# One attention head group of layer 1 as columns in every batch row, with one-piece copies, half-wise query spreading, earlier weight tails and new engine orders

## The chip, the core and the metric

The kernel runs on one core of a Trainium2 chip. The core has a matrix engine (TensorE, PE in the profile; its weight loads are PEld), a vector engine (VectorE, DVE), a scalar engine (ScalarE, ACT), GpSimd (POOL), and a sync engine (SyncE, SP) that here only starts DMA transfers. The engines run their own instruction streams in order and meet at semaphores. Matrix results go to PSUM, eight banks of 128 x 512 f32; all else lies in SBUF with 128 partitions.

The metric is the time of one execution on the device, in microseconds (us). A program is run several times; the median is compared.

## What is computed

Two layers, each attention over a cache and then a feed-forward block, with the same weights and the same cache in both layers. Eight batch rows, one token each, D = 448, 16 query heads on 8 cache heads ("kvh"), head size 256, and a window of the last 1024 of 4096 cached keys.

```python
def _A_ref(x, k_cache, v_cache, wq, wo):
    B, Sq, D = x.shape
    Hq, Dh = 16, 256
    Hkv, Sk = k_cache.shape[1], k_cache.shape[2]
    W = min(4096, max(256, Sk // 4))
    rep = Hq // Hkv
    q = (x @ wq).reshape(B, Sq, Hq, Dh).transpose(0, 2, 1, 3)
    k = jnp.repeat(k_cache[:, :, Sk - W:, :], rep, axis=1)
    v = jnp.repeat(v_cache[:, :, Sk - W:, :], rep, axis=1)
    scores = jnp.einsum("bhqd,bhkd->bhqk", q, k) * (Dh ** -0.5)
    o = jnp.einsum("bhqk,bhkd->bhqd", _softmax(scores), v)
    return o.transpose(0, 2, 1, 3).reshape(B, Sq, Hq * Dh) @ wo
...
x = A_x
x = x + _A_ref(_layernorm(x), A_k_cache, A_v_cache, A_wq, A_wo)
x = x + silu(_layernorm(x) @ B_w1) @ B_w2
x = x + _A_ref(_layernorm(x), A_k_cache, A_v_cache, A_wq, A_wo)
x = x + silu(_layernorm(x) @ B_w1) @ B_w2
```

## The kernel before

**Loads.** A batch row needs 8 K blocks and 8 V blocks, one of 512 KB for each kvh. They go through a ring of 30 SBUF slots, all started by SP in a fixed order (`pump`, `load_kv`, line 446): K 0 to 7 of row 0, V 0 to 7, K of row 1 and so on. Load n may start once the block 30 loads earlier has been read for the last time. Layer 2 uses the same blocks, so K block k of row b comes free when row b's layer-2 scores have read it, and the loads that wait for the first four K blocks of row b are V 6 and V 7 of row b+1 and K 0 and K 1 of row b+2. The weights are loaded once: `load_wq` (three pieces and a tail of 64 + 64 partitions), then `load_w2` and `load_wo` behind K of row 0, `load_w1` with its tail behind V of row 0. The tails are two DMAs each (`load_tail`, line 389). The input `x` is started by ACT.

**A batch row.** In what follows a name with @b is the work of row b.

- Layer 1: VectorE transposes the K blocks in place (line 599, names KW0 to KW7). `scores(b, 0, k2)` (line 614, S0.0 and S0.1, four groups of eight matmuls each for kvh 0 to 3 and 4 to 7), `softmax` (max0, exp0, perm0, turn0, l0, rl0), then the values. `pv_rows1` does kvh 0 to 3 (line 669, PV0), `pv_tiles1` kvh 4 to 7 one by one (line 680, PV4 to PV7). Each of the two ends in `o_turn`: ACT copies the PSUM bank (line 650, oev0, oevt), four matmuls turn it (line 651, oT0, oTt), VectorE scales it by the softmax sums (line 654, oTev0, oTevt). `wo_rows` (line 742, four groups of eight matmuls) multiplies with `wo` into bank XB; ACT copies the result row (line 776, rowb1), `fold` (line 481) turns it into columns and adds it to the residual in bank YB, and `xcols` (line 785, xb1) makes the layer's output x.
- `chain(b)`: statistics (line 793), `up` (line 806, w1), the second product (line 886, w2), copy (rowb2), fold, xb2, statistics; then `query_rows` makes the layer-2 queries: `wq` matmuls (line 858), a transpose on VectorE (line 511, qT), a product with a mask (line 865, qm), four matmuls that spread them (line 869, qd), two ACT copies (line 874, qbd2.0 and qbd2.1).
- Layer 2: `scores(b, 1, k2)` (also line 614, S1.0 and S1.1), softmax, `pv_rows2` (line 720, PV1.0 and PV1.1), `o_turn` (oev1, oT1, oTev1). What follows layer-2 attention is done for rows 0 to 6 together in `final_rows` and for row 7 in `final_last`.

**Row 7 is special before the change** (`LAST`). Its kvh 7 of layer 1 doesn't go through `pv_tiles1`. `pv_cols1` (line 691, PVc) multiplies the V block as weights, so that the result stands in columns at once, VectorE scales it (line 696, oTc7), and `wo_cols` (lines 758 and 760, woc, 24 matmuls) adds it straight to the residual in YB, with no copy, no turn and no fold. And its row copies are split: ACT copies a first part, VectorE the rest (`row_out`, lines 769 to 772; `o_turn`, lines 646 and 648). The planner lets a reader of a PSUM bank wait for earlier readers of that bank on other engines, so the VectorE part starts after the ACT part:

```python
for k in reads:
    ...
    if k[0] == "bank":
        for r in self.readers.get(k, ()):
            if r.eng != eng:
                dep(r, False)
```

**Order.** `Plan` keeps the tasks in program order, and for each engine the string in `ORDER` says which of the remaining tasks comes next: a digit n takes the n-th remaining one. SP has no string; it follows program order. `IDLE` says how many idle matmuls (line 848, 128 x 512, result unused) stand ahead of each row's `chain` and query spreading. Decoded, PE's order from layer-2 scores of row 5 to the statistics of row 6 is:

```
S1.0@5 x4  S1.1@5 x4  perm0@6 l0@6  PV0@6 x2  PV4@6  l1@5 perm1@5  oT0@6  PV5@6
PV1.0@5 x2  PV6@6  PV1.1@5  PV7@6  wo@6 x2  oTt@6  PV1.1@5  wo@6 x2  oT1@5
fold1@6  stat1@6
```

## Time and profile before

| what | us |
|---|---|
| median of 3 runs (lowest, highest) | 234.12 (233.54, 236.55) |
| the profiled execution | 234.68 |
| its span, first to last instruction | 232.9 |
| PE busy | 166.7 |
| DVE busy | 149.9 |
| ACT busy | 66.6 |
| POOL busy | 22.8 |

The profiled execution took 234.68 us, of which 232.9 lie between its first and its last instruction. PE busy counts matmuls, which are pipelined: 72% busy isn't 72% of what the engine could do. The page cuts the span in 40 slices of 5.8 us and gives for each the busy tenths of each engine, the matrix engine's granted clock, and the DMA share and rate. The timeline view lists instructions with start, duration, engine, line, output and input, and in brackets how long the engine had been idle and what released it. The windows view gives busy time by stretch, then the granted clock, the DMA share and GB/s.

### The profile page before, as it was taken

What the parts mean: (1) busy time and instruction counts of PE and PEld (TensorE: products, weight loads), DVE (VectorE), ACT (ScalarE), POOL (GpSimd) and SP (SyncE); (2) the same over time, 40 slices, a digit from 0 to 9 for tenths busy, and PEclk for the clock granted to TensorE, in tenths of its full rate; (3) what the DMA queues carried; (4) which work ended last, traced back from release to release, by engine and by line L of the source; (5) the groups of instructions that cost most, each with busy time, mean ns of one, the idle gap of its engine ahead of it and who ended that gap; (6) DMA issues with size and microseconds to landing.
All of it is one profiled execution on the core that took longest, in us unless ns stands there. A gap on an engine that the chain in (4) does not pass through costs nothing.

```text
span 232.9 us, 7828 instructions
## 1 busy us (share of the span) xinstructions
PE 166.7 (72%) x3479; PEld 97.3 (42%) x3479; DVE 149.9 (64%) x356; ACT 66.6 (29%) x188; POOL 22.8 (10%) x41
## 2 busy tenths in 40 slices
PE   0000338197988888878786978889788889898885
PEld 0000334135354545354335534453545455466644
DVE  6328986996963994297358736951984596424742
ACT  2000153631223326232222223223323223223331
POOL 1000202011000200110011002001100200000200
PEclk9999999769799999999999999999999999999999
DMA  6999999999999998999999999999999999500000
GB/s 246 377 377 404 378 380 403 410 374 396 405 393 404 407 408 336 343 418 406 348 385 416 406 349 414 407 390 389 409 406 379 412 407 408 221 3 3 3 3 4
DMA packets 22631, 78.17 MB, mean 336 GB/s; under 512 B 2231, under 2 KB 5318, under 8 KB 22214
## 3 DMA queue, kind: packets, MB, share of 16 engines
q1 hardware_dynamic: 22582, 77.68, 86.1%
q8 instruction: 27, 0.44, 0.8%
q14 instruction: 6, 0.05, 0.1%
q10 hardware_dynamic: 16, 0.01, 0.0%
HBM read 77.67 MB, written 0.01 MB: 334 GB/s over the span
## 4 chain that ended last, share of the span: by engine, by line
PE 35%; DVE 23%; DMA 18%; SPq 17%; ACT 3%; issue 2%; DVEq 0%; ACTq 0%
DVE slot L599 15%; DMA slot<-in_A_k_cache_dram 15%; SPq L446 10%; PE bank L614 9%; PE bank L806 5%; SPq L404 4%; PE bank L720 4%; DMA slot<-in_A_v_cache_dram 3%; PE bank L669 3%; SPq L389 3%; PE bank L680 2%; PE bank L742 2%; PE bank L869 2%; DVE bank L511 1%; DVE mm L626 1%
## 5 line engine op out<-in xcount | busy, mean ns | idle before, releaser
L599 DVE STREAM_TRANSPOSE slot<-slot 128x1024 uint32<-128x1024 uint32 x64 | 76.8, 1226 | 9.7 <-DMA slot<-in_A_k_cache_dram 9.5
L614 PE MATMUL bank<-slot,qbd 128*8 128x256 bf16 (+1 forms) x1024 | 38.4, 285 | 2.1 <-POOL qbd L590 1.1
L614 PEld LDWEIGHTS bank<-slot,qbd 128*8 128x8 bf16 (+1 forms) x1024 | 26.1, 88 | 13.3 <-DVE slot L599 4.2
L799 POOL TENSOR_TENSOR fcols<-fcols 128x1 f32<-128x1 f32 x17 | 9.4, 554 | 103.2 <-ACT fcols L797 103.2
L654 DVE TENSOR_TENSOR q1s<-bank,q1s 128x16 bf16<-128x16 f32 (+2 forms) x25 | 4.3, 171 | 22.8 <-PE bank L651 22.7
L806 PE MATMUL bank<-xz,w_sb 128*128 128x56 bf16 (+1 forms) x522 | 17.5, 191 | 0.0
L742 PE MATMUL bank<-wo_sb,q1s 128*1 128x449 bf16 x284 | 16.8, 354 | 0.6 <-DVE spread L374 0.5
L626 DVE TENSOR_REDUCE mm<-bank 128x1 f32<-128x256 f32 x17 | 7.2, 424 | 15.0 <-PE bank L614 14.8
L590 POOL TENSOR_TENSOR qbd<-q1s,fcols 128x256 bf16<-128x256 bf16 x16 | 9.6, 614 | 70.5 <-PE bank L680 62.4
L650 ACT ACTIVATE obuf<-bank 128x512 bf16<-128x512 f32 x15 | 9.0, 597 | 25.5 <-PE bank L680 18.1
L806 PEld LDWEIGHTS bank<-xz,w_sb 128*128 128x128 bf16 (+1 forms) x522 | 15.9, 99 | 0.7
L720 PE MATMUL bank<-slot,qbd 128*8 128x512 bf16 (+1 forms) x224 | 16.2, 381 | 0.0
L858 PE MATMUL bank<-wq_sb,xz 128*2 128x512 bf16 x196 | 13.7, 390 | 2.3 <-DVE xz L785 2.1
L633 ACT ACTIVATE qbd<-bank,mm 128x256 bf16<-128x256 f32 x17 | 8.1, 474 | 21.4 <-DVE mm L630 18.3
L669 PE MATMUL bank<-slot,qbd 128*4 128x512 bf16 x128 | 9.2, 410 | 5.3 <-DVE mm L627 1.9
L425 DVE TENSOR_REDUCE slot<-wo_sb 128x6 f32<-128x2688 bf16 x4 | 11.7, 2928 | 2.0 <-DMA wo_sb<-in_A_wo_dram 2.0
L680 PE MATMUL bank<-slot,qbd 128*12 128x512 bf16 (+3 forms) x124 | 11.2, 391 | 1.7 <-DMA slot<-in_A_v_cache_dram 1.7
L519 PE MATMUL bank<-xb,cols 128*128 128x8 bf16 x4 | 0.3, 173 | 14.9 <-DVE fcols L330 14.9
L886 PE MATMUL bank<-w_sb,hT 128*1 128x449 bf16 x112 | 8.1, 379 | 2.8 <-DVE hT L841 2.8
L797 ACT ACTIVATE fcols<-bank,fcols 128x1 f32<-128x1 f32 x17 | 4.4, 262 | 18.9 <-PE bank L793 18.8
L641 DVE RECIPROCAL q1s<-bank 128x16 f32<-128x16 f32 (+1 forms) x17 | 4.0, 233 | 8.8 <-PE bank L639 8.8
L433 ACT ACTIVATE slot<-w_sb 128x448 bf16<-128x448 bf16 x6 | 3.5, 576 | 21.4 <-DMA w_sb<-in_B_w_dram 21.2
(170 smaller groups left out, 236.9 us busy)
## 6 DMA issues: line engine op xcount, KB each, us to landing
slot<-in_A_k_cache_dram SPq DMA_DIRECT2D x64, 512.0 KB, 9.6
slot<-in_A_v_cache_dram SPq DMA_DIRECT2D x64, 512.0 KB, 12.4
wo_sb<-in_A_wo_dram SPq DMA_DIRECT2D x1, 3584.0 KB, 29.3
wq_sb<-in_A_wq_dram SPq DMA_DIRECT2D x3, 1024.0 KB, 7.0
w_sb<-in_B_w_dram SPq DMA_DIRECT2D x1, 1568.0 KB, 19.6
w_sb<-in_B_w_dram SPq DMA_DIRECT2D x1, 1344.0 KB, 18.1
wq_sb<-in_A_wq_dram SPq DMA_DIRECT2D x2, 256.0 KB, 10.1
w_sb<-in_B_w_dram SPq DMA_DIRECT2D x2, 112.0 KB, 17.8
```

The source lines that it names most:

```text
L425: dve(lambda e, rows=rows, s=s: e.tensor_reduce(s, rows[:, :, R0:M1].rearrange("p c (a n) -> p c a n", a=2), AX.X, ALU.add, negate=True), ...
L446: dma(lambda e: e.dma_start(slots[s][:, :].rearrange("p (u d) -> p u d", d=DH), cache[b, kvh, S0:SK, :].rearrange("(p u) d -> p u d", p=P) ...
L590: pool(lambda e, k2=k2: e.tensor_tensor(qdata(0, k2), q1s[:, b, 64 * k2:64 * k2 + 64].rearrange("p (n r) -> p n r", r=2).unsqueeze(3) .bro ...
L599: dve(lambda e, v=v: e.transpose(v, v), SL(s), SL(s), b, "KW%d" % k)
L614: fns.append(lambda e, w=w, j=j, kv=kv, cb=cb, par=par: e.matmul(sc[32 * j:32 * j + up_to, 0:256], w, kv, start=(cb == 0 and par == 0), st ...
L626: dve(lambda e: e.tensor_reduce(m[:, 0:1], x, AX.X, ALU.max, negate=True), bk(sc), [("mm", L)], b, "max" + name)
L669: pe([lambda e, u=u, j=j: e.matmul(bank[OB[0]][32 * j:32 * j + 4, 0:512], keys2(0, u, j, 1), vals2(b, j, u), start=(u == 0), stop=(u == 3) ...
L680: pe([lambda e, t=t, kvh=kvh, m=m: e.matmul(bank[SC[0]][32 * t:32 * t + 4 * m, 0:512], keys2(0, t, kvh, m), vals2(b, kvh, t), start=True, ...
L720: pe([lambda e, u=u, j=j, k2=k2: e.matmul(bank[OB[1]][32 * j:32 * j + 8 - 4 * k2, 0:512], keys2(1, u, 4 * k2 + j, 2 - k2), vals2(b, 4 * k2 ...
L742: fns.append(lambda e, i=i, w=w, c0=c0: e.matmul(bank[XB][32 * (i % 4):32 * (i % 4) + 1, c0:c0 + D + 1], oT(i), w, start=(i < 4), stop=(i ...
L806: fns.append(lambda e: e.matmul(bank[bi][p0:p0 + m, XS * (f % 7):XS * (f % 7) + XS], view(w1_sb[:], off, [(2, m)]), xbt[0][:, c:c + 1].bro ...
L858: fns.append(lambda e, j=j, c=c, k2=k2, w=w: e.matmul(bank[XB][32 * j:32 * j + 2, :], w, view(wq_sb[:], c * HD + (4 * k2 + j) * 512, [(64, ...
```

## The change

- **Layer 1's kvh 7 in columns in every row.** `last` becomes True for all rows, so `pv_tiles1` takes kvh 4 to 6, the last `wo_rows` group has four matmuls less, and `pv_cols1` and `wo_cols` follow, as row 7 had it. `xb1` now waits for `wo_cols` as well.
- **One-piece copies in row 7.** The split in `o_turn` and `row_out` goes; ACT copies all of it, as in the other rows.
- **Queries by halves.** In rows 0 to 6 the mask product, the four spreading matmuls and the ACT copy are done for each half (kvh 0 to 3, kvh 4 to 7) on its own: qm0, qd0, qbd2.0, then qm1, qd1, qbd2.1. The spreading matmuls write contiguous columns, and the ACT copy reads PSUM with a stride instead. Row 7, which had halves already, takes the same layout.
- **Weight tails first, on two queues.** The tails of `wq` and `w1` are started at the very beginning, lower partitions by SP and upper ones by ACT; `x` moves from ACT to SP, ahead of them.
- **New orders** on all four engines, and eleven idle matmuls become two (both in row 0).

Decoded, PE's order in the same stretch is now:

```
S1.0@5 x4  qd1@5  perm0@6 l0@6  S1.1@5 x4  PV0@6 x2  PV4@6 PV5@6  oT0@6  perm1@5
wo@6  PV6@6  PV1.0@5 x2  PV1.1@5  l1@5  oTt@6  wo@6 x3  PVc@6  PV1.1@5  fold1@6
woc@6  oT1@5  stat1@6
```

In row 0 the new orders put VectorE's work for the first queries ahead of most K transposes of row 0; `xb1@0` stands behind KW0@1 on VectorE in both orders.

```diff
-IDLE = {0: (7, 1), 1: (0, 0), 2: (1, 0), 3: (0, 0), 4: (1, 0), 5: (0, 0), 6: (1, 0), 7: (0, 0)}
+IDLE = {0: (2, 0), 1: (0, 0), 2: (0, 0), 3: (0, 0), 4: (0, 0), 5: (0, 0), 6: (0, 0), 7: (0, 0)}
...
-        dma(lambda e: e.dma_start(xrow, x2), ["xrow"], "x", via="act")
+        dma(lambda e: e.dma_start(xrow, x2), ["xrow"], "x")
+
+    def load_tails():
+        for n, (w, src, m, key) in enumerate(((wq_sb[:, 3 * HD:], A_wq, HD2, "wq"), (w1_sb[:, 3 * F:], B_w1, F2, "w1"))):
+            for h in range(2):
+                dma(lambda e, w=w, src=src, m=m, h=h: e.dma_start(w[64 * h:64 * h + 64, :],
+                                                                  src[3 * P:D, h * m:(h + 1) * m]),
+                    [(key, 3 + h)], "%st%d" % (key, h), via=("sp", "act")[h])
...
-        if b == LAST and name != "0":
-            act(lambda e: e.activation(buf[:, 0:256], bank[src][:, 0:256], ACTF.Copy), bk(src), keys_b[0:1], b,
-                "oeva" + name)
-            dve(lambda e: e.tensor_copy(buf[:, 256:512], bank[src][:, 256:512]), bk(src), keys_b[1:2], b, "oevd" + name)
-        else:
-            act(lambda e: e.activation(buf, bank[src][:, 0:512], ACTF.Copy), bk(src), keys_b, b, "oev" + name)
+        act(lambda e: e.activation(buf, bank[src][:, 0:512], ACTF.Copy), bk(src), keys_b, b, "oev" + name)
...
+        for k2 in range(2):
+            dve(lambda e, k2=k2: e.tensor_tensor(
+                qm[:, 64 * k2:64 * k2 + 64].rearrange("p (j n r) -> p j n r", j=4, r=2),
+                view(bank[XB][:], k2, [(0, 4), (32, 8), (256, 2)]), view(rmask, 0, [(1, 4), (0, 8), (0, 2)]), ALU.mult),
+                bk(XB) + ["rmask"], [("qm", k2)], b, "qm%d" % k2)
...
+    def spread_q(b, k2):
+        pe([lambda e, q=q, k2=k2: e.matmul(
+            bank[LB[1]][:, 256 * k2 + 64 * q:256 * k2 + 64 * q + 64], spread[:, 96 - 32 * q:224 - 32 * q],
+            qm[:, 64 * k2:64 * k2 + 64], start=True, stop=True, skip_group_check=True) for q in range(4)],
+            [("qm", k2)] + SPREAD, bk(LB[1]), b, "qd%d" % k2)
+        act(lambda e, k2=k2: e.activation(qbd[1][:, 8 + 256 * k2:264 + 256 * k2].rearrange("p (t q) -> p t q", q=4),
+                                          view(bank[LB[1]][:], 256 * k2, [(1, 64), (64, 4)]),
+                                          ACTF.Copy), bk(LB[1]), QB(1, k2), b, "qbd2.%d" % k2)
...
-        row_out(b, rhalf, ["rhalf"], "2")
+        act(lambda e: e.activation(rowb, bank[XB][:, 0:D + 2], ACTF.Copy, scale=rhalf), bk(XB) + ["rhalf"],
+            ROWB, b, "rowb2")
+        fold(b, ROWB, "2")
...
     load_x()
+    load_tails()
     load_wq()
...
-        last = b == LAST
+        last = True
```

More of the change, by code (lines that the diff above doesn't have):

```diff
@@ L25 @@
[L25 to L27 removed]
+        "oBknfldjrnt2567mg1d6ajfmnikkj1nfhj43f38fc74cc42507223444477466db8a449253464e533081161110082520141112"
+        "007066004a099007066660500020100088106600aa09900066667600000100088006600aa099007066666000020119080066"
@@ L220, in bass_interleave_layers__sliding_block_cached__dense_activation_silu__decode_kernel @@
     R = 30
-    RS = 200
     XC = 5
@@ L395, in load_wq @@
                 [("wq", c)], "wq%d" % c)
-        load_tail(wq_sb[:, 3 * HD:], A_wq, HD2, "wq")
     def load_w1():
@@ L914, in chain @@
             dve(lambda e, k2=k2, bi=bi: e.tensor_tensor(
[L915 to L916 removed]
+                qm[:, 64 * k2:64 * k2 + 64].rearrange("p (j n r) -> p j n r", j=4, r=2),
+                view(bank[bi][:], 0, [(0, 4), (32, 8), (1, 2)]), view(rmask, 0, [(1, 4), (0, 8), (0, 2)]), ALU.mult),
                 bk(bi) + ["rmask"], [("qm", k2)], b, "qm%d" % k2)
             (k2 == 1) and idle(b, 1, "idleX")
[L919 to L924 removed]
+            spread_q(b, k2)
     def final_rows(s):
@@ L1015, in final_last @@
                     [("q1s", b) if i0 else ("q1s", b, 0)], "woL")
-        row_out(b, 1.0, [], "L")
+        act(lambda e: e.activation(rowb, bank[XB][:, 0:D + 2], ACTF.Copy), bk(XB), [("rowb", 0), ("rowb", 1)], b, "rowbL")
+        fold(b, [("rowb", 0), ("rowb", 1)], "L")
         xcols(b, "L")
@@ L1089, in values1 @@
                     [("oT1", b, 2 * g)] + [("oT1", b, 2 * g + 1)] * (not (last and g == 3)), "wo")
-        row_out(b, 1.0, [], "1")
+        act(lambda e: e.activation(rowb, bank[XB][:, 0:D + 2], ACTF.Copy), bk(XB), ROWB, b, "rowb1")
+        fold(b, ROWB, "1")
         if last:
```

58 lines of the change are left out of this document (11 added, 47 removed).

## Prediction

> **What bounds the kernel now.** I read the page's slices first, then the chain of waits, then single stretches in the timeline and windows views.
>
> ```profile
> span 232.9 us, 7828 instructions
> GB/s 246 377 377 404 378 380 403 410 374 396 405 393 404 407 408 336 343 418 406 348 385 416 406 349 414 407 390 389 409 406 379 412 407 408 221 3 3 3 3 4
> PE 35%; DVE 23%; DMA 18%; SPq 17%; ACT 3%; issue 2%; DVEq 0%; ACTq 0%
> ```
>
> Loads run for 34 to 35 of the 40 slices of 5.8 us; then comes a tail of some 30 us without them. The load rate isn't level: it falls to 336 to 349 GB/s about once per batch row. The chain of waits passes through PE, DVE, DMA and SP in turn, so no single engine is the bound. It is a loop through the ring of slots, which one turn shows (row 5 to row 6):
>
> ```profile
> 165.24 0.21 DVE L785 SCALAR_TENSOR_TENSOR xz<-bank,fcols 128x5 bf16<-128x5 f32 x1
> 176.15 0.81 SPq L446 DMA_DIRECT2D slot<-in_A_v_cache_dram  x2
> 181.82 0.10 PEld L680 LDWEIGHTS bank<-slot,qbd 128*4 128x4 bf16 x4 [0.16 <-DMA slot<-in_A_v_cache_dram]
> 182.43 0.60 ACT L650 ACTIVATE obuf<-bank 128x512 bf16<-128x512 f32 x1 [2.52 <-PE bank L680]
> 183.70 0.93 PE L742 MATMUL bank<-wo_sb,q1s 128*1 128x449 bf16 x16
> 184.69 0.55 ACT L776 ACTIVATE obuf<-bank 128x450 bf16<-128x450 f32 x1 [0.17 <-PE bank L742]
> 185.29 0.26 PE L481 MATMUL bank<-cols,obuf 128*128 128x56 bf16 x3 [0.45 <-ACT obuf L776]
> 185.75 0.21 DVE L785 SCALAR_TENSOR_TENSOR xz<-bank,fcols 128x5 bf16<-128x5 f32 x1
> ```
>
> x of row 5 is ready at 165.45. 10.70 us later layer 2's first scores have read four K blocks, and SP may start V 6 and V 7 of row 6 (176.15). V 7 lands at 181.82, 5.67 us on, and PE waits for it (PV7). Copy, turn, `wo`, copy and fold follow, and x of row 6 is ready at 185.96, 4.14 us after the landing. Sum 20.51 us. What the channel needs for a row, and what rows take on average:
>
> ```profile
> 165.50:176.20 10.70, 9.51 (x229) 6.09 (x233) 9.14 (x16) 2.83 (x9) 1.11 (x2) 1.00 1.02 409
> 176.20:185.90 9.70, 8.16 (x152) 4.10 (x141) 4.46 (x15) 3.47 (x8) 1.20 (x2) 1.00 1.01 391
> 67.43 0.80 SPq L446 DMA_DIRECT2D slot<-in_A_v_cache_dram  x2
> 196.95 0.80 SPq L446 DMA_DIRECT2D slot<-in_A_v_cache_dram  x2
> ```
>
> Sixteen blocks of 512 KB are 8.39 MB, at 409 GB/s 20.5 us. From the start of V 6 of row 1 (67.43) to that of row 7 (196.95) six rows take 129.5 us, 21.6 each. So 1.1 us a row, 6.5 in all, is lost because the ring gives slots back too late, and any shortening of the loop is gained until 20.5 is reached. Row 5's turn is at that floor already; the average row isn't. PE has 1.54 us idle in the second stretch (9.70 less 8.16).
>
> **The change part by part.** The sum is made against the profiled execution's 234.68 us (span 232.9 and 1.8 around it), which is 0.56 above the median of 234.12.
>
> *Term A, the weight tails.*
>
> ```profile
> 8.00:12.00 4.00, 0.00 (x0) 0.00 (x0) 0.31 (x3) 0.00 (x0) 0.00 (x0) 1.00 1.01 345
> 16.00:20.00 4.00, 0.00 (x0) 0.00 (x0) 2.98 (x3) 0.00 (x0) 0.00 (x0) 1.00 1.03 410
> 44.00:48.00 4.00, 2.07 (x22) 1.44 (x23) 3.97 (x4) 2.09 (x9) 0.00 (x0) 0.50 1.03 413
> 48.00:52.00 4.00, 3.81 (x38) 1.04 (x36) 3.91 (x12) 0.74 (x2) 0.60 (x1) 0.67 1.04 364
> 2.15 1.45 SPq L389 DMA_DIRECT2D wq_sb<-in_A_wq_dram  x2
> ```
>
> Where the half-partition tails pass, the channel is fully busy and yet slower: 345 and 364 GB/s against 410. That is 0.63 + 0.45 = 1.1 us over the two stretches. With the halves in flight together the most to gain is 1.1; the least is a loss of 0.7, since `wq`'s first piece is now issued behind three short DMAs on SP (x and two tails; 1.45 / 2 = 0.7 us each for two such) and x alone doesn't fill the channel. I take -0.5, nearer the rows that show the slowness.
>
> The Trainium skill speaks against this (DMA: Bandwidth & Descriptors, "Rules for kernel authors"): transfers to two partition halves serialize on the same engines, from one queue or from two, and a second queue saves only issue time. By that rule the sum would be 229.1. The trace has no two halves in flight together from two queues.
>
> *Term B, the loop, in rows 1 to 6.* Row 7 has the column form before the change, so its price is in the trace:
>
> ```profile
> 201.77 0.09 PEld L680 LDWEIGHTS bank<-slot,qbd 128*4 128x4 bf16 x4 [0.18 <-DMA slot<-in_A_v_cache_dram]
> 202.36 0.39 ACT L646 ACTIVATE obuf<-bank 128x256 bf16<-128x256 f32 x1 [1.87 <-PE bank L680]
> 202.85 0.42 DVE L648 CAST obuf<-bank 128x256 bf16<-128x256 f32 x1 [0.54 <-ACT obuf L646]
> 204.82 0.34 ACT L772 ACTIVATE obuf<-bank 128x200 bf16<-128x200 f32 x1 [2.08 <-PE bank L742]
> 205.26 0.42 DVE L770 CAST obuf<-bank 128x250 bf16<-128x250 f32 x1 [1.39 <-PE bank L720]
> 205.13 0.59 PE L691 MATMUL bank<-qbd,slot 128*128 128x56 bf16 x16
> 206.15 0.30 PE L758 MATMUL bank<-q1s,wo_sb 128*128 128x56 bf16 x5
> 206.80 0.19 PE L760 MATMUL bank<-q1s,wo_sb 128*128 128x56 bf16 x1
> 207.02 0.23 DVE L785 SCALAR_TENSOR_TENSOR xz<-bank,fcols 128x5 bf16<-128x5 f32 x1 [0.50 <-PE bank L760]
> ```
>
> There V 6 is the last block that goes through copy, turn and fold. It lands at 201.77 and x is ready at 207.25, 5.48 us later. The split copies cost 202.36 to 203.27 and 204.82 to 205.68, 0.91 and 0.86, where one-piece copies take 0.60 and 0.55 (rows at 182.43 and 184.69): 0.62 of the 5.48 go, 4.86 remain. V 7 lands one block after V 6, 512 KB at 409 GB/s = 1.28 us, so x is ready 3.58 us after V 7 where rows 1 to 6 take 4.14. That is 0.56 less a row. V 7's own path is shorter still (columns 0.59, scaling, `wo` columns 0.84 from 206.15 to 206.99).
>
> The halves shorten the way from xb2 to S1.0:
>
> ```profile
> 194.72 0.61 PE L869 MATMUL bank<-qm,spread 128*128 128x128 bf16 x4
> 214.96 0.40 PE L919 MATMUL bank<-qm,spread 128*128 128x64 bf16 x4
> 194.37 0.29 DVE L865 TENSOR_TENSOR qm<-bank,fcols 128x128 bf16<-128x128 f32 x1
> 214.69 0.21 DVE L914 TENSOR_TENSOR qm<-bank,fcols 128x64 bf16<-128x64 f32 x1
> 195.37 0.66 ACT L874 ACTIVATE qbd<-bank 128x256 bf16<-128x256 f32 x2 [1.47 <-PE bank L869]
> ```
>
> A half spreads 0.21 us sooner and its mask product is 0.08 shorter. PE fills that time with S0.1 now, so I count 0.1. The ACT copy's strided PSUM read isn't in the trace; between nothing and double its 0.33 (0.66 / 2) I take nothing, since it reads as many elements. The second halves (0.40 on PE, 0.21 on DVE) stand beside S1.0, which doesn't need them.
>
> On PE a row pays 0.59 for PVc and 0.84 for woc and saves PV7 (0.61 at most, from its landing to the copy at 182.43; I count 0.4) and four of 16 `wo` matmuls (a quarter of 0.93): +0.8. The 1.54 us of idle covers that; if it doesn't, see the second rival. POOL's next masked queries now wait for PVc, and have until the second product of `chain`; no cost.
>
> Term B is (0.56 + 0.1) x 6 = -3.9 us, between 0 and the 6.5 that the floor allows.
>
> *Term C, row 7 up to x:* the same two copies, -0.6.
>
> *Term D, behind x of row 7.*
>
> ```profile
> 210.62 0.43 ACT L772 ACTIVATE obuf<-bank,fcols 128x200 bf16<-128x200 f32 x1 [0.99 <-PE bank L886]
> 211.15 0.48 DVE L769 TENSOR_SCALAR obuf<-bank,fcols 128x250 bf16<-128x250 f32 x1 [0.65 <-ACT obuf L772]
> 222.37 0.39 ACT L646 ACTIVATE qbd<-bank 128x256 bf16<-128x256 f32 x1 [0.48 <-PE bank L705]
> 222.93 0.41 DVE L648 CAST qbd<-bank 128x256 bf16<-128x256 f32 x1
> 189.41 0.64 ACT L776 ACTIVATE obuf<-bank,fcols 128x450 bf16<-128x450 f32 x1 [0.98 <-PE bank L886]
> ```
>
> rowb2: 210.62 to 211.63, 1.01, becomes 0.64. oev1b: 222.37 to 223.34, 0.97, becomes 0.60. The last row copy saves 0.31 as rowb1 does. Sum -1.05; from -0.4 (the new order puts the other rows' `wo` work ahead of fold2@7) to -1.3.
>
> *At nothing:* row 0's new order and the idle matmuls that go. x of row 0 needs KW0@1, which waits for a K block:
>
> ```profile
> 54.72 1.25 DVE L599 STREAM_TRANSPOSE slot<-slot 128x1024 uint32<-128x1024 uint32 x1 [1.50 <-DMA slot<-in_A_k_cache_dram]
> ```
>
> Work ahead of it is covered by the loads. The granted clock is 0.50 and 0.67 there even with idle matmuls (44 to 52). If a cold clock reached the later rows it would add to the second rival. From 67.43 on the channel isn't ahead of the ring, and that cover is gone.
>
> Sum: 234.68 - 0.5 - 3.9 - 0.6 - 1.05 = 228.6 us.
>
> **The rivals.**
>
> *The loop doesn't shorten.* In the new order PV1.0, half of PV1.1 and l1 of the previous row stand between PV6 and oTt; PE would wait 0.60 for the copy anyway, but these 24 matmuls may take longer. For: PE keeps order, and DVE is busy 9.14 of 10.70 us in the first stretch. Against: the same work stood between V 7 and x in part (PV1.1 before `wo`), and in row 7, with columns, 4.86 us remain. Then B is 0: 232.5. Chance 0.33.
>
> *PE becomes the bound, and the kernel slower.* If woc and PVc find PE without idle time between S1.0 and x, each of seven rows is longer by their 0.8, 5.6 in all, and B is lost: 234.68 + 5.6 - 2.15 = 238.1. It decides once fillers and a cold clock use up the 1.54 us of idle. Against: PE is at 8.16 of 9.70, clock 1.00. Chance 0.08.
>
> *All rows reach the floor:* B = -6.5, A = -1.1, D = -1.3: 225.2. For it: the shortened turn, 20.51 - 0.66 = 19.85, is under 20.5, so that late slots can be caught up. Against: the rate falls in every row. Chance 0.09.
>
> *The tails gain nothing* (A = 0, a mechanism of this kernel by itself: a busy channel moves the same half-partition packets wherever they stand): 229.1. Chance 0.4 within each of the others; it decides none of them. This is what the skill's rule above would give.
>
> **How the numbers follow.** The likeliest case, 228.6, has 0.50; with its own bounds 226.5 to 231. The range 225.2 to 234.2 takes in the first and third rival and leaves out the slower one and the corners, some 0.15. Measurements of this kernel tell 2% from no change, 229.4 on the median. Most of the likeliest case (0.38 of 0.50) and all of the third rival (0.09) lie below: 0.47, to which the profiled run's 0.56 above the median adds a little; I say 0.49. Slower by over 2% (238.8) needs the second rival at its worst: 0.04. The rest, 0.47, is within 2%.
>
> **What would show it.** A: 410 GB/s where 8 to 12 and 48 to 52 us had 345 and 364. B: starts of V 6 some 20.9 us apart, no slice under 370 GB/s after the start, and x ready about 3.6 us after V 7's landing. C and D: ACT copies of 0.55 to 0.64 in row 7 and no VectorE part. Wrong: PE without idle time between S1.0 and x with starts still 21.6 apart (first rival), or over 22 (second).

## The result, and the profile after

| | before | after |
|---|---|---|
| median of 20 runs of each in one session | 235.12 | 231.69 (230.38 to 234.99) |
| the profiled execution | 234.68 | 231.36 |
| its span | 232.9 | 229.5 |

The ratio after to before is 0.9858, 95% interval [0.9833, 0.9884]: 1.4% faster, within the 2% that count as the same. The time lies inside the range, 3 us above the predicted 228.6. The page of the changed kernel: span, rate by slice of 5.7 us, the instruction queue among the DMA queues, and the shares of the chain that ended last.

```profile
span 229.5 us, 8308 instructions
...
GB/s 173 416 406 406 380 381 397 409 417 413 407 407 405 407 408 396 415 406 407 366 411 408 363 331 411 411 399 356 416 410 401 409 406 405 261 3 4 3 3 4
...
q8 instruction: 29, 0.48, 0.9%
...
PE 33%; DMA 27%; SPq 20%; DVE 13%; ACT 3%; issue 2%; DVEq 0%; ACTq 0%
```

The rate still falls below 370 in four slices (366, 363, 331, 356). Two starts of V 6 cut the span into three parts that can be compared between kernels. The timeline of the changed kernel has rows 1 and 7:

```profile
65.80 0.80 SPq L445 DMA_DIRECT2D slot<-in_A_v_cache_dram  x2
...
194.93 0.80 SPq L445 DMA_DIRECT2D slot<-in_A_v_cache_dram  x2
```

| part of the span | before | after | difference | predicted |
|---|---|---|---|---|
| up to V 6 of row 1 | 67.43 | 65.80 | -1.6 | -0.5 (A) |
| six turns of the loop | 129.5 | 129.1 | -0.4 | -3.9 (B) |
| from V 6 of row 7 to the end | 35.9 | 34.6 | -1.4 | -1.65 (C, D) |

So the loop, which was to give two thirds of the gain, gave almost nothing, and the start gave three times what was forecast. The windows view of the changed kernel (busy time of PE, PEld, DVE, ACT, POOL, then granted clock, DMA share, GB/s) answers to A, and to the floor of the loop:

```profile
4.00:8.00 4.00, 0.36 (x5) 0.29 (x5) 2.88 (x29) 0.00 (x0) 0.00 (x0) 1.00 1.03 346
8.00:12.00 4.00, 0.41 (x12) 0.40 (x12) 2.57 (x20) 0.23 (x1) 0.00 (x0) 1.00 1.00 418
...
48.00:52.00 4.00, 4.00 (x58) 1.85 (x54) 3.25 (x8) 2.36 (x10) 0.00 (x0) 1.00 1.03 419
...
163.00:173.30 10.30, 9.11 (x221) 5.58 (x221) 9.32 (x16) 2.62 (x9) 2.26 (x4) 1.00 1.02 409
173.30:183.60 10.30, 9.14 (x189) 4.92 (x187) 5.21 (x15) 3.58 (x9) 0.61 (x1) 1.00 1.02 406
```

All four tails have now landed by 6.3 us, in stretches at 131 and 346 GB/s (0 to 4 and 4 to 8 us; 164 and 422 before), and the stretch at 48 to 52 is at 419 instead of 364. Over the first 16 us both kernels move the same 5.2 MB, so the gain shows at 48 to 56, where the tail of `w1` passed before. K 0 of row 1 lands at 53.74, 1.0 us sooner than before (54.70). A landing, here and below, is the last of the sixteen updates with which the DMA engines report one block.

**One turn of the loop after the change.** The timeline from V 6 of row 6, which lands at 178.09, to x of row 6:

```profile
178.13 0.39 PE L674 MATMUL bank<-slot,qbd 128*4 128x512 bf16 x4
...
178.35 1.47 PE L714 MATMUL bank<-slot,qbd 128*8 128x512 bf16 x24
178.58 0.60 ACT L644 ACTIVATE obuf<-bank 128x512 bf16<-128x512 f32 x1 [1.31 <-PE bank L674]
...
179.99 0.24 PE L645 MATMUL bank<-selb,obuf 128*128 128x6 bf16 x4
...
180.16 1.12 PE L736 MATMUL bank<-wo_sb,q1s 128*1 128x449 bf16 x20
...
181.34 0.55 ACT L1074 ACTIVATE obuf<-bank 128x450 bf16<-128x450 f32 x1 [2.17 <-PE bank L736]
...
181.73 0.61 PE L714 MATMUL bank<-slot,qbd 128*4 128x512 bf16 x8
...
182.28 0.26 PE L480 MATMUL bank<-cols,obuf 128*128 128x56 bf16 x3
...
183.39 0.23 DVE L764 SCALAR_TENSOR_TENSOR xz<-bank,fcols 128x5 bf16<-128x5 f32 x1 [0.20 <-PE bank L754]
...
183.77 0.28 PE L772 MATMUL bank<-xz 128*128 128x56 bf16 x4 [0.33 <-DVE q1s L648]
```

The copy (L644) ends at 179.18, and the turn (L645) starts only at 179.99: 24 matmuls of the previous row's layer 2 (L714) and its sums hold PE 0.8 us beyond it. The row copy ends at 181.89, and the fold (L480) starts at 182.28, behind eight more of them. This is the mechanism of the first rival, 24 matmuls between PV6 and oTt, and it can be read off the rows.

The same for all rows, worked out from landings and rows (V 6 is the last block that takes the way through the copy):

```
mean of rows 1 to 6, us            before   after   row 7 after
V 6 landed to start of its copy      -      1.09       1.18
start of that copy to x ready        -      4.86       4.06
V 6 landed to x ready               5.94    5.96       5.24
V 7 landed to x ready               4.39    4.31       4.01
x ready to start of the next V 6   10.94   10.70
start of V 6 to V 7 landed          6.25    6.51
```

From V 7 to x the rows gained 0.08 us, not 0.56. The 0.24 gained from x to the next start was lost again between the start of V 6 and V 7's landing. What the prediction took from row 7, which has less work of other rows in the way (16 matmuls of layer 2 behind PV6 in place of 24, and four short ones ahead of the fold in place of eight), doesn't hold in rows 1 to 6: there the way from the copy to x takes 0.8 us more (4.86 against 4.06), and that's the fillers. Besides, PE is busy with other work when V 6 of rows 2, 4 and 5 lands and comes to it 1.33, 1.46 and 0.65 us later.

**Row 7.** The copies are single (0.60, 0.55, 0.64), with no VectorE part:

```profile
200.66 0.60 ACT L644 ACTIVATE obuf<-bank 128x512 bf16<-128x512 f32 x1 [2.17 <-PE bank L674]
...
202.77 0.55 ACT L1074 ACTIVATE obuf<-bank 128x450 bf16<-128x450 f32 x1 [0.65 <-PE bank L736]
...
204.48 0.23 DVE L764 SCALAR_TENSOR_TENSOR xz<-bank,fcols 128x5 bf16<-128x5 f32 x1 [0.93 <-PE bank L754]
...
208.18 0.64 ACT L875 ACTIVATE obuf<-bank,fcols 128x450 bf16<-128x450 f32 x1 [0.99 <-PE bank L871]
```

x is ready at 204.72, and 24.8 us follow to the end, where 25.6 followed before (207.25 to 232.9): D gave -0.9. From the start of V 6 to x it is 9.8 us, 10.3 before: C gave -0.5.

### The profile page after: what moved, and what is told of

Its sections match the earlier page's. It is cut to its first block, busy times and chain, and to the rows that moved or that the text cites. A ratio compares the mean times of both kernels' runs of the same rounds, so it can differ in the third digit from the quotient of the medians.

```text
span 229.5 us, 8308 instructions
## 1 busy us (share of the span) xinstructions
PE 166.5 (73%) x3722; PEld 101.1 (44%) x3722; DVE 150.9 (66%) x364; ACT 67.4 (29%) x188; POOL 22.6 (10%) x41
## 4 chain that ended last, share of the span: by engine, by line
PE 33%; DMA 27%; SPq 20%; DVE 13%; ACT 3%; issue 2%; DVEq 0%; ACTq 0%
DMA slot<-in_A_k_cache_dram 18%; SPq L445 14%; DMA slot<-in_A_v_cache_dram 9%; DVE slot L598 9%; PE bank L613 7%; PE bank L736 4%; PE bank L714 4%; SPq L403 3%; PE bank L785 3%; PE bank L663 2%; PE bank L674 2%; ACT qbd L632 1%; PE bank L685 1%; PE bank L854 1%; PE bank L645 1%
## 5 line engine op out<-in xcount | busy, mean ns | idle before, releaser
L613 PE MATMUL bank<-slot,qbd 128*8 128x256 bf16 (+1 forms) x1024 | 40.8, 285 | 5.7 <-DVE slot L598 3.4
L613 PEld LDWEIGHTS bank<-slot,qbd 128*8 128x8 bf16 (+1 forms) x1024 | 24.5, 88 | 15.3 <-DVE slot L598 5.7
L644 ACT ACTIVATE obuf<-bank 128x512 bf16<-128x512 f32 x17 | 10.1, 596 | 24.7 <-PE bank L674 12.5
L785 PE MATMUL bank<-xz,w_sb 128*128 128x56 bf16 (+1 forms) x522 | 17.0, 189 | 0.0
L714 PE MATMUL bank<-slot,qbd 128*8 128x512 bf16 (+1 forms) x224 | 15.4, 380 | 0.0
L736 PE MATMUL bank<-wo_sb,q1s 128*1 128x449 bf16 x256 | 15.1, 353 | 0.1
L636 DVE STREAM_TRANSPOSE qbd<-bank 128x256 bf16<-128x256 bf16 x17 | 7.4, 434 | 7.9 <-PE bank L634 7.9
L674 PE MATMUL bank<-slot,qbd 128*12 128x512 bf16 (+2 forms) x96 | 9.8, 413 | 2.5 <-DVE q1s L640 1.7
L858 ACT ACTIVATE qbd<-bank 128x256 bf16<-128x256 f32 x16 | 6.1, 383 | 15.5 <-PE bank L854 15.5
L776 ACT ACTIVATE fcols<-bank,fcols 128x1 f32<-128x1 f32 x17 | 4.5, 262 | 20.9 <-PE bank L772 20.9
```

Source lines behind the costliest of these rows:

```text
L613: fns.append(lambda e, w=w, j=j, kv=kv, cb=cb, par=par: e.matmul(sc[32 * j:32 * j + up_to, 0:256], w, kv, start=(cb == 0 and par == 0), st ...
L644: act(lambda e: e.activation(buf, bank[src][:, 0:512], ACTF.Copy), bk(src), keys_b, b, "oev" + name)
L674: pe([lambda e, t=t, kvh=kvh, m=m: e.matmul(bank[SC[0]][32 * t:32 * t + 4 * m, 0:512], keys2(0, t, kvh, m), vals2(b, kvh, t), start=True, ...
L714: pe([lambda e, u=u, j=j, k2=k2: e.matmul(bank[OB[1]][32 * j:32 * j + 8 - 4 * k2, 0:512], keys2(1, u, 4 * k2 + j, 2 - k2), vals2(b, 4 * k2 ...
L736: fns.append(lambda e, i=i, w=w, c0=c0: e.matmul(bank[XB][32 * (i % 4):32 * (i % 4) + 1, c0:c0 + D + 1], oT(i), w, start=(i < 4), stop=(i ...
L785: fns.append(lambda e: e.matmul(bank[bi][p0:p0 + m, XS * (f % 7):XS * (f % 7) + XS], view(w1_sb[:], off, [(2, m)]), xbt[0][:, c:c + 1].bro ...
```

## The experiments

Ratios are to the kernel before, run on the same chip in the same session. "Start", "loop" and "end" are the three parts of the span above, from each kernel's profiled execution. For the two combined kernels only the ratio is used.

| kernel | ratio, 95% interval | start | loop | end |
|---|---|---|---|---|
| before | 1 | 67.4 | 129.5 | 35.9 |
| after | 0.9858 [0.9833, 0.9884] | 65.8 | 129.1 | 34.6 |
| tails alone | 0.9930 [0.9889, 0.9971] | 67.2 | 129.4 | 35.9 |
| one-piece copies alone | 0.9940 [0.9897, 0.9982] | 68.8 | 129.8 | 34.9 |
| no idle matmuls alone | 0.9943 [0.9897, 0.9988] | 67.2 | 130.2 | 36.1 |
| columns alone | 1.0111 [1.0061, 1.0161] | 67.2 | 132.3 | 36.0 |
| after without columns | 1.0015 [0.9970, 1.0061] | 67.1 | 130.6 | 34.6 |
| tails and copies | 0.9957 [0.9912, 1.0003] | | | |
| tails, copies, no idle matmuls | 0.9882 [0.9812, 0.9953] | | | |
| after, other banks | 0.9871 [0.9828, 0.9914] | 66.0 | 128.7 | 34.6 |
| the same, fillers moved | 0.9994 [0.9958, 1.0030] | 65.8 | 131.3 | 34.6 |
| the same, VectorE's order changed too | 1.0464 [1.0405, 1.0523] | 66.5 | 143.9 | 34.8 |

The ends are the steadiest column: 35.9 to 36.1 with split copies, 34.9 with single ones and row 7's old order, 34.6 to 34.8 with the new order.

### The parts of the change by themselves

**Tails alone**, on the kernel before:

```diff
-        dma(lambda e: e.dma_start(xrow, x2), ["xrow"], "x", via="act")
+        dma(lambda e: e.dma_start(xrow, x2), ["xrow"], "x")
...
+    load_tails()
     load_wq()
```

> The kernel before with one part of the change alone: x on SP, the four weight tails first, on SP and ACT. In the changed kernel K 0 of row 1 landed 1.0 us sooner than before (53.7 against 54.7). Theory 1 (the tails moved that, and the loop through the ring hands it on to the end): K 0 of row 1 lands at 53.7, V 6 of row 1 starts about 0.5 to 1.0 us sooner than 67.4, the time falls by 0.6 to 1.0 us. Rival (half-partition transfers cost the same wherever they stand, and the 1.0 us came from elsewhere): K 0 of row 1 at 54.7, time unchanged within 0.3 us.

K 0 of row 1 lands at 53.67 (54.70 before), as much sooner as in the changed kernel, and the ratio is 0.993. But V 6 of row 1 starts only 0.3 us sooner (67.16), less than theory 1's 0.5 to 1.0. The timeline at x of row 0 says why:

```profile
53.94 1.23 DVE L599 STREAM_TRANSPOSE slot<-slot 128x1024 uint32<-128x1024 uint32 x1
...
55.11 0.55 ACT L776 ACTIVATE obuf<-bank 128x450 bf16<-128x450 f32 x1 [1.61 <-PE bank L742]
...
55.89 0.21 PE L486 MATMUL bank<-cols,obuf 128*128 128x56 bf16 x2
56.15 0.23 DVE L785 SCALAR_TENSOR_TENSOR xz<-bank,fcols 128x5 bf16<-128x5 f32 x1 [0.91 <-PE bank L486]
```

VectorE has transposed K 0 by 55.17, and x now waits for PE's fold, which ends at 56.10. In the changed kernel it's the other way round: the columns of row 0 are done at 54.31, and x follows the transpose of K 0:

```profile
53.77 1.25 DVE L598 STREAM_TRANSPOSE slot<-slot 128x1024 uint32<-128x1024 uint32 x1 [2.42 <-DMA slot<-in_A_k_cache_dram]
...
54.12 0.19 PE L754 MATMUL bank<-q1s,wo_sb 128*128 128x56 bf16 x1
54.94 0.20 DVE L764 SCALAR_TENSOR_TENSOR xz<-bank,fcols 128x5 bf16<-128x5 f32 x1
```

**One-piece copies alone**: the branches for row 7 in `o_turn` and `row_out` go, and their VectorE tasks with them.

```diff
-        if b == LAST and name != "0":
...
-        else:
-            act(lambda e: e.activation(buf, bank[src][:, 0:512], ACTF.Copy), bk(src), keys_b, b, "oev" + name)
+        act(lambda e: e.activation(buf, bank[src][:, 0:512], ACTF.Copy), bk(src), keys_b, b, "oev" + name)
...
-        if b == LAST:
+        if False:
```

> The kernel before with row 7's copies in one piece alone. Predicted for these copies: 0.6 us up to x of row 7 and 1.05 us behind it. Theory 1: the stretch from the start of V 6 of row 7 to the end falls by 1.4 to 1.65 us and so does the time. Rival (other work on PE covers the copies): less than 0.5 us.

The end is 34.9 us, 1.0 less than before, short of theory 1's 1.4 to 1.65 and above the rival's 0.5; the ratio is 0.994. The start of this one profile is 1.3 us later (68.8), though the edit doesn't touch rows 0 and 1: K 0 of row 1 landed at 55.43, and x to S1.0 took 11.87 us. So a start read from one profile can be off by that much.

**The changed kernel without the columns** (row tiles PV7 instead, in the same place):

```diff
-        last = True
+        last = b == LAST
```

> The changed kernel with layer 1's kvh 7 back in tiles in rows 0 to 6 (PV7 ahead of oTt, no PVc, no woc), the orders else as they are. Theory 1 (the columns gained nothing because PE works off layer 2's values between PV6 and oTt anyway): within 1 us of the changed kernel. Rival (columns do shorten V 7 to x by 0.56 a row, and something else in the new orders cost as much): 2.5 to 3.5 us slower than the changed kernel, about the time of before.

V 7's landing to x takes 5.18 us in the mean (4.31 with columns), the loop 1.5 us more, the start 1.3. Nothing is left of the gain: 1.0015. Theory 1 falls; in the new order the columns are worth 1.6%.

**The kernel before without idle matmuls**:

```diff
-IDLE = {0: (7, 1), 1: (0, 0), 2: (1, 0), 3: (0, 0), 4: (1, 0), 5: (0, 0), 6: (1, 0), 7: (0, 0)}
+IDLE = {0: (0, 0), 1: (0, 0), 2: (0, 0), 3: (0, 0), 4: (0, 0), 5: (0, 0), 6: (0, 0), 7: (0, 0)}
```

> The kernel before without its eleven idle matmuls, nothing else. Theory 1 (they neither hold the clock nor stand in the way for long): x of row 0 and V 6 of row 1 move by less than 0.3 us, time unchanged within 0.4 us. Rival a (they delay PE's row 0, part of the 1.6 us that the changed kernel is ahead at V 6 of row 1): 0.5 us or more faster at V 6 of row 1. Rival b (without them the clock stays low longer): w1 of row 0 takes over 2.35 us and the time grows by 0.5 us or more.

0.9943: they didn't help. V 6 of row 1 starts 0.2 us sooner, as theory 1 had it; the time fell by more than its 0.4 us (1.3 by the ratio, 0.3 to 2.4 by its interval), which no part of the profile shows. The granted clock at 44 to 52 us was 0.56 and 0.59 without them, 0.50 and 0.67 with them.

**Columns alone**, in the old order (the last three lines are the orders, decoded):

```diff
-        last = b == LAST
+        last = True
...
+PE, rows 0 to 6: PVc@b directly behind oTt@b, woc@b directly behind fold1@b
-PE, rows 0 to 6: PV7@b
+DVE, rows 0 to 6: oTc7@b directly behind oTevt@b
```

> The kernel before, with the last kvh of layer 1 as columns in rows 0 to 6 too, everything else in the old order: PV7's row tiles go, its columns follow directly behind oTt, the wo columns directly behind fold1, the copy of the columns directly behind the copy of the turn. Theory 1 (the columns shorten the way from V 7's landing to x as the prediction had it, and in the changed kernel the new order's fillers, PV1.0, PV1.1 and l1 between PV6 and oTt, ate most of it): V 7's landing to x falls from 4.40 us to 3.6 to 3.9 in the mean of rows 1 to 6, starts of V 6 come 21.1 to 21.3 apart (21.6 before), and the time is 0.984 to 0.99 of the kernel before. Rival (PE has no room for the columns' extra 0.8 us a row when the rest of the order stays as it was; the new order is what makes the columns pay): V 7's landing to x stays at 4.3 or more, starts stay 21.5 apart, time 0.995 to 1.005.

Slower, 1.0111; V 7's landing to x is 4.74, the loop 132.3. The rival had the direction right, but the size is beyond it, and its reason isn't seen: between the start of V 6 and x PE has at least 1.5 us idle in every row (row 6, 178.20 to 188.80 us: 10.60 less 9.00 busy). The timeline at row 3, whose V 6 lands at 116.34:

```profile
117.14 0.39 PE L680 MATMUL bank<-slot,qbd 128*4 128x512 bf16 x4
...
117.48 1.48 PE L720 MATMUL bank<-slot,qbd 128*8 128x512 bf16 x24
117.58 0.60 ACT L650 ACTIVATE obuf<-bank 128x512 bf16<-128x512 f32 x1 [2.59 <-PE bank L680]
118.89 0.17 PEld L651 LDWEIGHTS bank<-selb,obuf 128*128 128x128 bf16 x4 [0.43 <-issue]
```

Here too 24 matmuls stand behind PV6, and the turn comes 0.7 us after the copy's end (118.18). With row tiles, those fillers passed the time until V 7 landed; with columns V 7 isn't awaited there any more, and the fillers stand in V 6's way. So the columns don't pay by themselves, and the new order without them ends at 1.0015 although it has the tails and the single copies; in these two tests the columns and the order pay only together.

**Tails and copies together** (the first two diffs), no other part:

> The kernel before with two parts of the change alone: the weight tails on both queues (x on SP's), and row 7's copies in one piece. Orders, idle matmuls, row tiles and masked queries as before. Theory 1 (columns, halves and the new orders of rows 1 to 6 come to nothing between them; the whole gain of the change is that of these two parts): 0.985 to 0.990 of the kernel before, no different from the changed kernel's 0.986; starts of V 6 from row 1 to row 7 stay 129.3 to 129.6 us apart. Rival (the two parts don't add up, and the loop's work carries about half of the gain): 0.991 to 0.996.

0.9957, in the rival's range: both together gave no more than each alone, within the intervals, and theory 1 (the whole gain is theirs) falls: the changed kernel's 0.9858 lies outside the interval. Columns, halves, orders and the idle matmuls that went carry the other 1%. The start column shows one place where they and the tails need each other. With the tails alone V 6 of row 1 starts at 67.16, with columns alone (tails late) at 67.18, with tails and new orders but no columns at 67.10; with both, in four kernels, at 65.80 to 66.48. K 0's landing and PE's work of row 0 end close together, so that each can hide the other's gain. These are single profiles, and the one-piece copies show how far such a start can move by itself; what the columns do to x of row 0 can be read in the rows above.

**The same without idle matmuls** (the fourth diff too):

> The former kernel without any idle matmuls. Theory 1 (PE doesn't need them here, and each filler only stands in the way: without them alone the kernel before ran at 0.9943): the three parts add up, 0.979 to 0.984 of the kernel before, faster than the changed kernel. Rival (the idle matmuls matter only where the tails were late, so that their gain and that of the tails are the same microsecond at K 0 of row 1): 0.985 to 0.989.

0.9882 with a wide interval that reaches into both expectations and takes in the changed kernel's 0.9858. Whether the idle matmuls' gain adds to the tails' stays open, and with it whether the columns, halves and orders give anything that tails, copies and idle matmuls don't give without them.

### Can the loop be shortened?

**Other banks.** In the turn of row 6, stat1 waits 0.33 us for VectorE's copy of the previous row's turn, since both stand in bank LB[1].

```diff
-        sbk, col = (YB, 6 * XS) if name == "2" else (LB[1], 400)
+        sbk, col = (YB, 6 * XS) if name == "2" else (LB[0 if b < LAST else 1], 400)
...
-            bi = (XB, OB[1])[h]
+            bi = (XB, OB[0 if b < LAST else 1])[h]
```

> The changed kernel with its orders, but the sums for layer 1's statistics (stat1) stand in bank LB[0] and the second half of up in OB[0] for rows 0 to 6, so that stat1 no longer shares a bank with the turn of the previous row's layer 2 (oT1) and needn't wait for VectorE's copy of it. Theory 1 (that wait, 0.33 us behind x in the turn of row 5 to row 6, is on the loop): x to S1.0 falls from 10.70 to 10.4 in the mean, the loop of six rows from 129.1 to 127.5, time 0.992 to 0.995 of the changed kernel, 0.978 to 0.982 of the kernel before. Rival (something else is late next at this place, or the loop takes it up elsewhere): no change, 0.984 to 0.988 of the kernel before.

0.9871, no different from the changed kernel. x to S1.0 fell by 0.12, the loop by 0.4: the rival.

**Fillers moved** out of the stretch ahead of x, in rows 1 to 6 (row 6's order is shown; layer 2's copies on ScalarE and VectorE move back with them):

```diff
-PE:  PV6@6  PV1.0@5 x2  PV1.1@5  l1@5  oTt@6  wo@6 x3  PVc@6  PV1.1@5  fold1@6  woc@6  oT1@5  stat1@6
+PE:  PV6@6  wo@6  PV1.0@5  oTt@6  PV1.0@5  wo@6 x2  PVc@6  l1@5  fold1@6  woc@6  PV1.1@5  stat1@6  w1@6 x2  PV1.1@5
```

> The former kernel (statistics in LB[0]) with the fillers moved in rows 1 to 6: of the previous row's PV1.0 and PV1.1 only one PV1.0 stands between PV6 and oTt, l1 goes between PVc and fold1, PV1.1 behind the wo columns and behind w1, oT1 behind the first scores of the next row; ScalarE's copy of layer 2's values goes ahead of rowb2, VectorE's behind xb2. Theory 1 (the fillers between V 6 and x are what kept the way from V 7's landing to x at 4.31 us): that way falls to 3.6 to 3.9, starts of V 6 come 21.0 to 21.2 apart, time 0.985 to 0.992 of the changed kernel, 0.972 to 0.978 of the kernel before. Rival (work is only moved: what leaves the stretch ahead of x comes back in the stretch from x to S1.0 or holds V slots longer): V 7's landing to x falls, x to S1.0 grows by as much or S1.0 to V 7's landing does, time 0.984 to 0.99 of the kernel before.

Slower than the changed kernel, 0.9994, and beyond the rival's 0.99 too. V 7's landing to x was 4.05 to 5.24 in single rows, 4.52 in the mean. The timeline of row 5 shows what took the fillers' place (V 7 lands at 160.00):

```profile
160.26 0.59 PE L685 MATMUL bank<-qbd,slot 128*128 128x56 bf16 x16
...
161.29 1.25 DVE L598 STREAM_TRANSPOSE slot<-slot 128x1024 uint32<-128x1024 uint32 x1 [1.87 <-DMA slot<-in_A_k_cache_dram]
162.46 0.12 DVE L690 TENSOR_TENSOR q1s<-bank,q1s 128x4 bf16<-128x4 f32 x1
162.63 0.20 PEld L752 LDWEIGHTS bank<-q1s,wo_sb 128*128 128x128 bf16 x5 [1.37 <-DVE q1s L690]
...
163.85 0.20 DVE L764 SCALAR_TENSOR_TENSOR xz<-bank,fcols 128x5 bf16<-128x5 f32 x1
```

The columns (L685) were ready at 160.85. VectorE's order has a transpose of the next row's K ahead of their copy (L690), that transpose waited 1.87 us for its block, and PE's `wo` columns (L752) waited 1.37 us behind it.

**VectorE's order fitted to it**: the copy of the columns first, one transpose ahead of x, the others spread further back (row 4's order; on PE the last S0.1 goes behind qd0 where it stood ahead).

```diff
-DVE: oTevt@4  KW0@5  oTc7@4  KW1@5  xb1@4  KW2@5 KW3@5  hT@4 x2  KW4@5 KW5@5  xb2@4  rl1@3 oTev1@3  KW6@5 KW7@5  qT@4  qm0@4
+DVE: oTevt@4  oTc7@4  KW0@5  xb1@4  KW1@5 KW2@5  hT@4 x2  KW3@5 KW4@5  xb2@4  KW5@5 KW6@5  rl1@3 oTev1@3  qT@4  qm0@4  KW7@5
```

> The kernel with moved fillers (x2_fill), and VectorE's order made to fit it in rows 1 to 6: the copy of the columns' turn (oTc7) directly behind the turn's copy, one transpose of the next row's K before x instead of two, two each behind x, the hidden layer and xb2, the last behind the first mask product. In x2_fill x was ready on PE up to 1.6 us before VectorE, busy with a 1.25 us transpose, wrote it. Theory 1 (VectorE's order is what held x there, and V 7's landing to x can come near to the prediction's 3.6): V 7's landing to x is 3.7 to 4.0 in the mean of rows 1 to 6, starts of V 6 come 20.9 to 21.2 apart, time 0.974 to 0.981 of the kernel before. Rival (PE comes late to V 6, so x can't be earlier, and later transposes hold up the scores): V 7's landing to x 4.2 or more or x to S1.0 over 11, time 0.985 to 1.0.

Far slower, 1.0464, beyond the rival's 1.0 too. The way from the copy to x is now 4.06 to 4.07 us in each of rows 1 to 6, the 4.06 of row 7, so it was the fillers that made it 4.86 and VectorE's order that kept it long once they were moved. Row 1 alone shows that the whole predicted way exists: V 7 to x 3.73 us, V 6 to x 5.00 (predicted 3.58 and 4.86); in the other rows PE came late to V 6. But x to S1.0 grew from 10.70 to 14.17. The timeline of that stretch (row 1 to row 2):

```profile
86.30 1.23 DVE L598 STREAM_TRANSPOSE slot<-slot 128x1024 uint32<-128x1024 uint32 x1
...
87.59 0.89 PE L613 MATMUL bank<-slot,qbd 128*8 128x256 bf16 x16 [2.38 <-DVE slot L598]
...
91.47 0.80 SPq L445 DMA_DIRECT2D slot<-in_A_v_cache_dram  x2
```

PE stands 2.38 us for the transposes that were pushed back, with all that follows in its order. VectorE has 9.3 us of work in the 10.3 us behind x (the window 163.0 to 173.3 above): a transpose of 1.25 us that leaves the stretch ahead of x has no room behind it. The granted clock was lower too (0.93 in the mean of the profiled execution, 1.00 in the changed kernel's), so not all of the loss need be the order's.

### What the channel itself needs

Two programs hold the loads alone, at most six blocks outstanding; the output is zeros. One has 2,800 matmuls beside them that depend on no load, the other none.

```diff
+    loads = [t for t in pl.tasks if t.eng == "sp" and not t.name.startswith("out")]
...
+    for i, t in enumerate(loads[6:]):
+        t.deps[loads[i].idx] = (loads[i], True)
...
+        for g in range(N_MM // 56):
+            pe([lambda e: e.matmul(bank[0][:, 0:56], ident[:], ident[:, 0:56], start=True, stop=True,
+                                   skip_group_check=True)] * 56, ["ident"], bk(0), 0, "mm")
```

> Loads alone (the same transfers in the same order, at most six blocks outstanding, no wait for any engine), and 2,800 matmuls of 56 columns on PE that depend on no load; nothing of attention or of the layers is computed and the output is zeros. It asks what the channel itself needs for a row of 16 blocks while PE fetches instructions. Theory 1 (the channel's own rate is 409 GB/s, and the instruction fetches only make single blocks late): 20.4 to 20.6 us for 16 blocks, the spread between a block's first and last landing update jumps by about 1 us at each fetch. Rival (the fetches cost the channel itself): 21 us or more, so that the floor of the loop lies above 20.5.

> The same loads as in d_loadpe, with no matmuls, so that hardly any instructions are fetched; nothing is computed and the output is zeros. Theory 1 (instruction fetches take one DMA engine for about 1.05 us each, and a block lands only with its slowest engine): V 7 of row 7 lands 1 to 3 us earlier than the 198.5 of d_loadpe, and the spread of a block's landing updates stays level. Rival (the slow landings come from the memory, not from fetches): within 0.3 us of 198.5, with jumps of the spread as before.

The windows of the program without matmuls (DVE, POOL, clock, DMA share, GB/s):

```profile
72.00:92.40 20.40, 0.00 (x0) 0.00 (x0) 1.00 1.02 409
...
112.90:133.40 20.50, 0.00 (x0) 0.00 (x0) 1.00 1.03 410
```

The one with matmuls, whose page has 21 instruction packets (0.34 MB in all), the last of them at 132.4 us:

```profile
72.00:92.40 20.40, 12.73 (x402) 12.45 (x402) 0.00 (x0) 0.00 (x0) 0.88 1.03 407
92.40:112.90 20.50, 15.04 (x477) 14.77 (x474) 0.00 (x0) 0.00 (x0) 0.87 1.02 404
112.90:133.40 20.50, 12.31 (x413) 12.04 (x409) 0.00 (x0) 0.00 (x0) 0.92 1.02 400
133.40:153.90 20.50, 0.81 (x25) 0.60 (x21) 0.00 (x0) 0.00 (x0) 0.63 1.02 409
```

```
                                       no matmuls   matmuls   before   after
V 7 of row 7 lands, us                    194.9      198.5    202.97   200.71
row 1's V 7 to row 7's, per row            20.50      20.69    21.52    21.30
from first to last update of a block    0.57-0.74    3.3-4.85   1.2-3.4  1.0-2.9
```

(The spreads are those from V 3 of row 1 on.) The floor of 20.5 us a row that the prediction used is right for loads alone. With matmuls the last block lands 3.6 us later, more than the "1 to 3" of theory 1. But the loss doesn't come at each fetch, as the first of the two expectations had it. Set against the program without matmuls, the landings fall back in three steps: 1.0 us behind the fetch at 8.53, 1.4 behind that at 58.04 and 1.4 behind that at 107.65, every eighth of the 21. The 18 others delay no landing by over 0.1 us, and 0.2 us is made up in row 4. So from V 7 to V 7 rows 2 and 4 take 20.47 and 20.46 us with their fetches, row 3 takes 21.84, and the mean of the three is 20.9. By this estimate 0.2 to 0.4 of the 1.0 us that a row of the kernel before lay above the floor wasn't the ring's to give; no run shows what the fetches cost inside the kernel itself.

## Why the prediction came out as it did

- **What bounds the kernel**: a loop through the ring, with the starts of V 6 as its marks. That reading held, and the three parts of the span account for the 3.4 us between the two spans. The floor left out the instruction fetches, 0.2 to 0.4 us a row by the estimate above. And the load rate's falls to 336 to 349 GB/s come at three places, not "about once per batch row".
- **The number**: 231.69 is inside the range, but outside the likeliest case's own bounds (226.5 to 231) and nearer to the first rival's 232.5 than to 228.6. That it came as near as it did is luck: the largest term failed, and the start gave 1.1 us more than its term, out of things that were counted at nothing.
- **A, the tails, -0.5**: direction right, size wrong. K 0 of row 1 lands 1.0 us sooner and the start of the loop comes 1.6 us sooner. The prediction treated row 0 as covered by the loads. That cover was thin: PE's row 0 ended 0.6 us ahead of x before the change (L486 at 55.31, x at 55.93), and without the columns it ends after K 0 once K 0 is early. So the columns of row 0, counted at nothing, let the tails' gain through: with early tails x of row 0 is ready at 55.13 with columns and at 56.62 without. The other 0.6 us is x to S1.0 of row 0, 11.28 before and 10.66 after, and most of it goes along with the granted clock: the two profiles with 0.69 and 0.65 at 56 to 60 us (before, and one-piece copies alone) took 11.28 and 11.87, those with the old order and 1.00 there 10.78 to 10.94, those with the new order 10.46 to 10.66. That leaves 0.1 to 0.5 us for row 0's new order and halves; no run separates these two.
- **The skill's rule against it.** By the Trainium skill (DMA: Bandwidth & Descriptors, "Rules for kernel authors") two transfers to partition halves serialize, from one queue or from two. The trace doesn't speak against it: where the halves pass, the rate is 346 GB/s after and 345 before, and the first 16 us move as much as before. The gain sits at 48 to 56 us (364 and 384 GB/s before, 419 and 415 after; 0.8 us at 409), so the place of the tails can have made it; no run separates the queues from the place.
- **B, the loop, -3.9**: this is the step that failed. Its term was "x is ready 3.58 us after V 7", taken from row 7 by way of V 6's 4.86, and set against the 4.14 of row 6, where the mean of rows 1 to 6 was 4.39. Rows 1 to 6 took 4.31 from V 7 and 5.96 from V 6. What row 7 has less of is the work of other rows: in rows 1 to 6 the 24 matmuls between PV6 and oTt, and eight ahead of the fold, make the way from the copy to x 4.86 (4.06 in row 7, 4.27 in the prediction). That's the first rival as it was written down, and the last experiment on the loop, where the way fell to 4.06 with the fillers moved and VectorE's order fitted, shows it. Up to the copy it was 1.09 us where the prediction had 0.59, since PE came late to V 6 in three rows. The first rival's 232.5, with the start's further 1.1 and the end's 0.3 put right, would be 231.7. The sum has no term for VectorE ahead of x; the moved fillers showed it next in line, at 1.25 us a piece.
- **B's other piece, 0.1 from the halves**: x to S1.0 fell by 0.24, and the start of V 6 to V 7's landing grew by 0.26. No run has the halves by themselves. The second isn't explained by one cause; V 7 landed 2.76 and 2.02 us behind V 6 in rows 4 and 5, not the 1.28 of the prediction, and instruction fetches at the time of SP's issue are seen in single rows (below).
- **PE's extra 0.8 us, covered by the 1.54 of idle**: true in the new order, with 1.16 us idle in the second stretch (10.30 less 9.14). In the old order PE had idle time too, 1.55 to 2.47 us between the start of V 6 and x with columns alone, and yet that kernel lost 1.1%. So the second rival's condition, PE without idle time, came about in neither; what counts is what stands ahead of the turn.
- **C and D, -1.65**: -1.4 measured. The copies alone gave -1.0 of it, the new order of row 7 the rest; C came as -0.5, D as -0.9.

What stays open: why tails and copies together gained no more than either alone, although their places in the span (start and end) don't touch. The loop of single profiles with the old order varies by 0.8 us (129.4 to 130.2), which is as much as each part is worth. And the tails, the copies and the idle matmuls alone each gave 0.993 to 0.994, some 1.3 to 1.6 us, while their profiled spans (232.5, 233.4 and 233.5 us) are 0.4 less to 0.6 more than the 232.9 before. So the split of the 1.4% among the parts of the change isn't settled.

## What to carry to other kernels

A way measured in the last row, where less of other rows' work is in flight, is a lower bound for the same way in the rows before it: add the work of other rows that the order puts between its steps. When a wait goes, the work that filled it has to be moved too, on every engine, or it stands in the way; the columns cost 1.1% with the old order and gained 1.6% with the new one. And two things that end within a microsecond of each other can hide each other's gain: try such edits together as well as alone.

## What wasn't expected of the hardware

**A few instruction fetches delay loads.** A fetch is one packet of 16 KB on the instruction queue. It takes 1.07 us in the median (0.93 to 1.41 in the changed kernel), and a block of 512 KB has landed with the last of its sixteen updates. With no matmuls the sixteen updates of a block lie 0.57 to 0.74 us apart all through. With them they lie 1.9 us apart before the fetch at 58.04 and 3.3 behind it, 3.45 before that at 107.65 and 4.85 behind it, and twelve blocks later 3.6 again. These are the steps by which the landings fall back, and the fetches between them cost nothing that can be seen. That would fit one DMA engine that lags and is hit again by every eighth fetch; the trace doesn't tell which engine took a packet, so this isn't shown. Spread evenly over the channel, 0.34 MB would cost 0.8 us at 409 GB/s; it cost 3.6. The Trainium skill (Runtime: NRT & Kernel Launch, "Instruction fetch mechanics") calls the cost of crossing a 16 KiB boundary mostly hidden. The trace agrees in the size of the packets and for 18 of the 21 fetches; the three others cost the loads 1.0 to 1.4 us each. The column form raised the count from 7828 instructions to 8308 and the fetches from 27 to 29; the changed kernel without columns has 7854 and 27.

**SP's issue is delayed at such times too.** Starts of one block take SP 0.43 us in the median. In the changed kernel the start of V 7 of row 4, at 131.20, took 1.50 us, with a fetch at 131.23, and V 7 landed 2.8 us after V 6 instead of 1.3. That isn't the only cause of long starts: those between 39 and 55 us take 1.0 to 1.7 us each, with no fetch in that stretch.

**The clock.** At 44 to 52 us the profile of the changed kernel shows a granted clock of 1.00 with two idle matmuls, and that of the kernel before 0.50 and 0.67 with eight ahead of row 0's layer 2. But the idle matmuls don't decide it: with the tails alone, and the same eight, it was 1.00, and with other banks, and two, it was 0.50. Over its 20 runs the changed kernel's mean granted clock goes from 0.96 to 1.00. No run says why.
